# The last 64 tokens of two batches mixed in the two column halves of TensorE's array, with refitted load estimates

## Chip, core and metric

One core of a Trainium2 chip. The metric is the device time of one execution in microseconds. Engine names: PE is TensorE, PEld its weight loads, DVE is VectorE, ACT is ScalarE, POOL is GpSimd, SP is SyncE.

## The reference, cut to what matters

Eight batches of 576 tokens go through block-causal attention (8 heads of 64), and the result x through a mixer:

```python
h = np.maximum(xt @ w_tok1, 0.0) @ w_tok2      # xt: x with tokens and channels swapped
u = x + h.transpose(0, 2, 1)                   # token mixing: 576 tokens <- 256 hidden
h2 = np.maximum(u @ w_ch1, 0.0) @ w_ch2        # channel mixing
return u + h2
```

Token mixing has 576 output tokens, which are 4 chunks of 128 and a rest of 64. The rests of two batches (a pair) share one tile of 128 rows, `um`, so that channel mixing treats them as one more chunk.

## The kernel before

All work is put down as operations with a cost, a priority and dependencies; a list scheduler in the kernel then lays them out, and the order that it finds is the program order of every engine. Loads count in it with an estimated transfer time (`xfer`). The rest of each batch is mixed alone, by two matmuls with the whole array. Of their 128 output rows only 64 are used; the weights are padded with zeros, or shifted by 64 columns for an odd batch, so that the used rows lie where `um` wants them:

```python
for si in range(4 if b == 0 else 0, 5):            # si == 4 is the rest of 64 tokens
    def emit(o, si=si, bank=bank):
        c0 = 128 * si - (64 if si == 4 and odd else 0)
        for t in range(NDT):                       # NDT = 2 halves of the contraction
            nc.tensor.matmul(out=bank_of(bank), lhsT=w2_sb[:, t, c0 : c0 + 128],
                             rhs=at[:, t, :], start=(t == 0), stop=(t == NDT - 1))
    op = P.add("PE", mm_cost(512, 2), emit, ...)
    # then VectorE: u (or 64 rows of um) = bank + x
```

The attention scores use the array in another way: four heads lie in four groups of 32 rows, and their matmuls run side by side. The scheduler knows this as `mode=1` and charges 0.1 us for each change of mode. And at the start PE is given work on zeros (16 matmuls of 512 columns, then smaller ones) to raise its clock before the first scores.

The softmax here doesn't subtract the row's maximum and nothing guards it: scores larger than these inputs give would overflow.

Of the kernel before, what the change touches and what calls it, by code (L numbers as in the profile page):

```python
# [152 lines left out]
def kernel(  # L153
# [53 lines left out]
    zeros = sb.tile([128, 512], BF16, name="zeros")  # L207
    w1_sb = sb.tile([128, 5, DT], BF16, name="w1_sb")
    w1o_sb = sb.tile([128, DT], BF16, name="w1o_sb")
    w2_sb = sb.tile([128, NDT, 640], BF16, name="w2_sb")  # L210
    wc1_sb = sb.tile([128, NDM, DC], BF16, name="wc1_sb")
    wc2_sb = sb.tile([128, NDC, DM], BF16, name="wc2_sb")

# [36 lines left out]
    def init_tiles():  # L250
        def fill(engine, key, prio, *parts):
            for t, value in parts:
                def emit(o, t=t, value=value):
                    (nc.vector if engine == "DVE" else nc.gpsimd).memset(t, value)

                pads.setdefault(key, []).append(P.add(engine, 0.17, emit, (), prio))

        for i, t in enumerate(kT):
            fill("DVE", ("kT", i), -1e4 + i, (t[:, S:640, :], 0.0))
        for i in range(2):  # L260
            fill(
                "DVE", ("v", i), -60 + 20 * i,
                (v1[i][64:128, 4, :, :], 0.0),
                (v1[i][:, 0:4, :, 64:65], 1.0),
                (v1[i][0:64, 4, :, 64:65], 1.0),
            )
            fill("DVE", ("e", i), -70, (e_sb[i][:, :, 1536:1600], 0.0))
            fill("DVE", ("et", i), -70, (et_sb[i], 0.0))
            fill("DVE", ("um", i), -70, (um_sb[i], 0.0))
        fill("DVE", "zeros", -1e5, (zeros, 0.0))  # L270
        fill("DVE", "w1", -70, (w1_sb[64:128, 4, :], 0.0), (w1o_sb[0:64, :], 0.0))
        fill("DVE", "w2", -70, (w2_sb[:, :, S:640], 0.0))

        def emit(o):
            make_identity(nc, ident)

        pads["ident"] = [P.add("POOL", 0.6, emit, (), -1e6)]
# [39 lines left out]
    def load_qk(b, hg, after=[]):  # L317
        i = (2 * b + hg) % 3
        first = b == 0 and hg == 0
        prio = 10 * b + 4 * hg - (100 if b == 0 else 0)  # L320
        parts = ((0, NB // 2), (NB // 2, NB))
        done = []
        for n, (src, raw, dst) in enumerate(((k, kraw[i], kT[i]), (q, qraw[i], qT[i]))):
            hbm = src[b, 4 * hg : 4 * hg + 4].rearrange("h (p k) d -> (h p) (k d)", p=32)
            raw2 = raw.rearrange("p k d -> p (k d)")

            st = stage[0][:, 1152 * n : 1152 * (n + 1)]
            raw_war = reuse(("raw", n, i))
            T_war = reuse(("T", n, i))
            loads = []  # L330
            if not first:
                def emit_load(o, hbm=hbm, raw2=raw2):
                    nc.gpsimd.dma_start(out=raw2, in_=hbm)  # L333

                loads = [P.add("POOL", 0.55, emit_load, raw_war, prio + n, xfer=8 * 0.191)]
            for f, (k0, k1) in enumerate(parts):
                if first:
                    def emit_load(o, k0=k0, k1=k1, hbm=hbm, st=st):
                        queue = nc.sync if o.engine == "SP" else nc.scalar
                        queue.dma_start(out=st[:, D * k0 : D * k1], in_=hbm[:, D * k0 : D * k1])  # L340

                    ld = P.add(("SP", "ACT")[f % 2], 0.45, emit_load, (), -1e4 + n, xfer=(k1 - k0) * 0.1)

                    def emit_cast(o, k0=k0, k1=k1, raw2=raw2, st=st):
                        cast(o, raw2[:, D * k0 : D * k1], st[:, D * k0 : D * k1])

                    w = D * (k1 - k0)
                    ld = P.add(EVAC, {"ACT": act_cost(w), "DVE": dve_cost(w)}, emit_cast, [ld], -1e4 + 2 + n)
                    reads(("g", 0), ld)
                    loads = [ld]  # L350

                def emit(o, raw2=raw2, dst=dst, k0=k0, k1=k1):
                    nc.vector.transpose(  # L353
                        dst[:, 0:S, :]
                        .rearrange("p s e -> p (s e)")
                        .bitcast(I32)
                        .rearrange("p (a k) -> p k a", k=NB)[:, k0:k1],
                        raw2.bitcast(I32).rearrange("p (k a) -> p k a", k=NB)[:, k0:k1],
                    )

                op = P.add("DVE", 0.02 + 32 * (k1 - k0) * 0.00185, emit, loads + T_war + after, prio + 0.1 * n, urgent=(2, 0)[b] if b < 2 else -1)
                reads(("raw", n, i), op)
                done.append(op)
        return done

    def load_v(b):
# [5 lines left out]
        for hg in range(2) if b == 0 else (None,):  # L372
            hs = slice(0, H) if hg is None else slice(4 * hg, 4 * hg + 4)
            nh = hs.stop - hs.start
            for J in range(5):
# [7 lines left out]

                prio = (10 * b + (0, 5.7, 6)[min(b, 2)] if b else (-95.5, 5.15)[hg]) + 0.01 * J
                sw = reuse(("gs", J)) if staged and b else [] if staged else war
                op = P.add("POOL", 0.66 + 0.02 * nh, emit, sw, prio, xfer=p * nh / 16 * (0.0175 if staged else 0.0145))
                if staged:
                    def emit(o, st=st, dst=dst):
                        cast(o, dst, st)
# [8 lines left out]
    def load_token_weights():  # L398
        def load(dst, src, xfer, prio):
            def emit(o):  # L400
                nc.gpsimd.dma_start(out=dst, in_=src)

            return P.add("POOL", 0.66, emit, (), prio, xfer=xfer)

        done1 = [
            load(w1_sb[:, 0:4, :], moe_w_tok1[0:512, :].rearrange("(c p) t -> p c t", p=128), 32 * 0.06, 5.0),
            load(w1_sb[0:64, 4, :], moe_w_tok1[512:576, :], 4 * 0.06, 5.1),
        ]
        done2 = [
            load(w2_sb[:, :, 0:S], moe_w_tok2.rearrange("(p c) s -> p c s", c=2), 8 * 0.3, 5.2)  # L410
        ]
        done1o = [load(w1o_sb[64:128, :], moe_w_tok1[512:576, :], 4 * 0.06, 12.0)]
        return (done1 + pads["w1"], done1 + done1o + pads["w1"]), done2 + pads["w2"]

    def channels(cc):

# [2 lines left out]
    def load_channel_weights():  # L419
        done1, done2 = [[] for _ in range(NDC)], []  # L420
        for f in range(2):
            for m in range(NDM):
                def emit(o, m=m, f=f):
# [1 line left out]
                        out=wc1_sb[:, m, 768 * f : 768 * f + 768],  # L425
                        in_=moe_w_ch1[128 * m : 128 * (m + 1), 768 * f : 768 * f + 768],
                    )
                op = P.add("POOL", 0.53, emit, (), (6.0, 11.5)[f], xfer=0.98)
                for cc in range(0, 8) if f == 0 else range(4, NDC):
                    done1[cc].append(op)  # L430
        for c in range(0, NDC, 4):
# [330 lines left out]
    def token_mix(b, x_done, w1_ready, w2_ready):  # L762
# [4 lines left out]
        a_war = reuse(("a", b % 2))  # L767
        u_war = reuse(("u", b % 3))
        if not odd:
            um_free[pair] = reuse(("um", pair % 2)) + pads["um", pair % 2]  # L770
        uT_war = reuse(("uT", b % 2))
        u_done, done, um_done = [], [], []
        if b == 0:
# [6 lines left out]
        else:  # L780
            a_all = [
                token_up(b, slice(0, DM), (tt,), x_done, a_war, w1_ready, prio) for tt in range(NDT)
            ]
        for si in range(4 if b == 0 else 0, 5):
            bank = {}

            def emit(o, si=si, bank=bank):
                c0 = 128 * si - (64 if si == 4 and odd else 0)
                for t in range(NDT):
                    nc.tensor.matmul(  # L790
                        out=bank_of(bank),
                        lhsT=w2_sb[:, t, c0 : c0 + 128],
                        rhs=at[:, t, :],
                        start=(t == 0),
                        stop=(t == NDT - 1),
                    )

            op = P.add(
                "PE", mm_cost(512, 2), emit,
                a_all + w2_ready + (um_free[pair] if si == 4 else u_war), prio + 1 + 0.1 * si,  # L800
                take=[(BANK, bank)],
            )
            reads(("a", b % 2), op)

            def emit(o, si=si, bank=bank):
                if si < 4:
                    r, dst = slice(0, 128), ut[:, si, :]
                else:
                    r = slice(64, 128) if odd else slice(0, 64)
                    dst = umt[r, :]  # L810
                nc.vector.tensor_tensor(out=dst, in0=bank_of(bank)[r, :], in1=xt[r, si, :], op=ADD)  # L811

            op = P.add("DVE", dve_cost(512), emit, [op], prio, give=[bank])
            reads(("x", b % 3), op)
            u_done.append(op)


        crossbar = b >= 2
# [10 lines left out]
        if crossbar and odd:  # L829
            def emit(o):  # L830
                nc.sync.dma_start_transpose(out=umT[pair % 2], in_=umt)

            op = P.add("SP", 1.0, emit, [u_done[4]] + reuse(("umT", pair % 2)) + um_first[pair], prio, xfer=1.0)
            reads(("um", pair % 2), op)
            um_done.append(op)
        for si in () if crossbar or b == 0 else range(4 + odd):
# [7 lines left out]
                        ps[:, 128 * m : 128 * (m + 1)], src[:, 128 * m : 128 * (m + 1)], ident  # L844
                    )

            deps = [u_done[si]] + pads["ident"]
            deps += uT_war if si < 4 else reuse(("umT", pair % 2)) + um_first[pair]
            op = P.add(
                "PE", mm_cost(128, 4), emit, deps, prio + 2 + 0.1 * si, take=[(BANK, bank)]  # L850
            )
# [11 lines left out]
                EVAC, {"ACT": act_cost(512), "DVE": dve_cost(512, 2)}, emit, [op], prio, give=[bank]  # L863
            )
            (done if si < 4 else um_done).append(op)
        if not odd:
            um_first[pair] = [u_done[-1]]
        return done, um_done, u_done

    um_first = {}  # L870
    um_free = {}


# [161 lines left out]
    for b in range(B + 1):  # L1035
# [7 lines left out]
            )  # L1043
        if b > 0:
            p = b - 1
            uT_done, um_done, u_done = token_mix(p, x_done[p], w1_ready, w2_ready)
            g_done = channel_up(p, uT_done, wc1_ready, 10 * p + 2)
            if p < B - 1:
                channel_down(p, g_done, wc2_ready, u_done, 10 * p + 4)
            if p % 2 == 1:  # L1050
                gm_done = channel_up_mixed(p // 2, um_done, wc1_ready, 10 * p + 3.5)
                prio = 10 * p + (5 if p < B - 1 else 3.9)
                channel_down(p, gm_done, wc2_ready, u_done, prio, mixed=True)
            if p == B - 1:
                channel_down(p, g_done, wc2_ready, u_done, 10 * p + 4)

# [33 lines left out]
```

## Time and profile before

| | before |
|---|---|
| median of the first 3 runs | 308.82 us (308.43 to 308.92) |
| median of those and the 3 beside the changed kernel | 308.63 us |
| span in the profile | 306.6 us |
| PE busy | 97% |
| mixing matmuls of rests | 16, each 0.216 us of PE's stream |
| changes between whole array and score sets | 118 |

The profile's lines are shown and read in the prediction.

### The profile page before, as it was taken

To read this page: it belongs to the slowest core of one execution; us is meant where nothing else is said; L and a number is where in the kernel's file an instruction comes from. 1 tells how busy PE (TensorE), PEld (TensorE's weight loads), DVE (VectorE), ACT (ScalarE), POOL (GpSimd) and SP (SyncE) were. 2 spreads that over 40 slices of the span, in tenths; PEclk is the share of its full clock that TensorE was granted. 3 is DMA by queue.
4 is the path that set the end of the run, shared out by engine and by line. 5 is a ranking of instruction groups with operands and counts; after the bars stand their busy time and mean duration, and the time that the engine had idled before them with its cause. 6 is when DMAs were issued, how large, how long until landed. Compare 5 with 4: busy or idle time off the path is not lost.

```text
span 306.6 us, 7153 instructions
## 1 busy us (share of the span) xinstructions
PE 298.7 (97%) x3007; PEld 162.1 (53%) x3036; DVE 154.6 (50%) x384; ACT 164.2 (54%) x232; POOL 62.1 (20%) x96
## 2 busy tenths in 40 slices
PE   8999999999999999999999999999999999999995
PEld 4575446464564554545545565455445645545643
DVE  6655719898684758856749545281033012011022
ACT  5885864767756645785674884505405602604600
POOL 8866353702600421330050000000000000000000
PEclk9999999999999999999999999999999999999999
DMA  8999999995994798793193030122311312111013
GB/s 201 157 200 208 206 189 181 227 214 88 112 127 74 148 139 135 129 99 71 68 81 87 0 71 2 71 77 45 66 71 71 69 68 83 22 68 72 0 34 138
DMA packets 64512, 31.95 MB, mean 104 GB/s; under 512 B 53088, under 2 KB 55264, under 8 KB 64480
## 3 DMA queue, kind: packets, MB, share of 16 engines
q0 software_dynamic: 44448, 17.34, 48.9%
q1 hardware_dynamic: 19744, 13.57, 16.3%
q10 hardware_dynamic: 288, 0.59, 0.6%
q8 instruction: 23, 0.38, 0.5%
q14 instruction: 9, 0.07, 0.1%
HBM read 35.85 MB, written 9.44 MB: 148 GB/s over the span
## 4 chain that ended last, share of the span: by engine, by line
PE 90%; DVE 6%; DMA 1%; issue 1%; ACT 1%; DVEq 0%
PE mm L966 28%; PE mm L882 27%; PE sc L468 9%; PE mm L515 8%; PE mm L696 6%; PE mm L790 5%; PE mm L909 4%; DVE kT L353 1%; DVE qT L353 1%; DMA gT<-in_k_dram 1%; DVE x_sb L543 1%; PE mm L740 0%; ACT e_sb L487 0%; PE mm L292 0%; PE mm L843 0%
## 5 line engine op out<-in xcount | busy, mean ns | idle before, releaser
L487 ACT ACTIVATE e_sb<-sc 128x1024 bf16<-128x1024 f32 x95 | 92.4, 1026 | 35.8 <-PE sc L468 35.0
L882 PE MATMUL mm<-uT,wc_sb 128*128 128x512 bf16 x384 | 88.5, 380 | 0.1
L966 PE MATMUL mm<-wc_sb,gT 128*128 128x512 bf16 (+1 forms) x378 | 86.3, 373 | 1.5 <-issue 0.8
L682 ACT ACTIVATE gT<-mm 128x512 bf16<-128x512 f32 x75 | 44.8, 597 | 64.6 <-PE mm L882 63.6
L882 PEld LDWEIGHTS <-wc_sb 128*128 128x128 bf16 x384 | 42.2, 114 | 39.7 <-issue 3.5
L966 PEld LDWEIGHTS <-gT 128*128 128x128 bf16 x396 | 36.8, 98 | 42.1 <-issue 4.2
L991 DVE TENSOR_TENSOR o_sb<-mm,u_sb 128x512 f32<-128x512 f32 (+1 forms) x29 | 19.5, 672 | 63.4 <-PE mm L966 63.0
L382 POOL DMA_DIRECT2D v<-in_v_dram x45 | 36.7, 836 | 25.9 <-PE sc L468 22.1
L468 PE MATMUL sc<-qT,kT 32*128 32x320 bf16 (+4 forms) x744 | 35.4, 281 | 1.1 <-DVE qT L353 1.0
L515 PEld LDWEIGHTS <-e_sb 128*128 128x128 bf16 x896 | 30.9, 97 | 7.8 <-issue 4.3
L515 PE MATMUL mm<-v,e_sb 128*128 128x65 bf16 x896 | 33.0, 193 | 0.2 <-DVE x_sb L543 0.2
L543 DVE TENSOR_TENSOR x_sb<-mm,rinv 128x320 bf16<-128x320 f32 x64 | 30.4, 487 | 1.7
L468 PEld LDWEIGHTS <-kT 32*128 32x128 bf16 x752 | 12.4, 93 | 19.8 <-issue 17.2
L493 DVE MEMSET e_sb<- 64x128 uint32 (+1 forms) x72 | 10.5, 153 | 24.3 <-ACT e_sb L487 20.9
L353 DVE STREAM_TRANSPOSE kT<-kraw 128x288 int32<-128x288 int32 x32 | 20.8, 707 | 3.6 <-PE sc L468 2.1
L811 DVE TENSOR_TENSOR u_sb<-mm,x_sb 128x512 bf16<-128x512 f32 x28 | 17.6, 684 | 9.0 <-PE mm L790 7.4
L353 DVE STREAM_TRANSPOSE qT<-qraw 128x288 int32<-128x288 int32 x32 | 21.0, 704 | 0.2
L696 PE MATMUL mm<-x_sb,w_sb 128*128 128x512 bf16 (+1 forms) x99 | 17.9, 314 | 0.3
L684 DVE TENSOR_SCALAR gT<-mm 128x512 bf16<-128x512 f32 x21 | 14.5, 689 | 6.8 <-PE mm L882 6.8
L790 PE MATMUL mm<-aT,w_sb 128*128 128x512 bf16 x70 | 17.7, 379 | 0.1
L333 POOL DMA_DIRECT2D kraw<-in_k_dram x15 | 8.3, 557 | 46.9 <-DVE kT L353 39.8
L537 DVE RECIPROCAL rinv<-mm 128x5 f32<-128x5 f32 x64 | 11.3, 184 | 7.5 <-PE mm L515 7.2
(66 smaller groups left out, 168.3 us busy)
## 6 DMA issues: line engine op xcount, KB each, us to landing
out_dram<-o_sb SPq DMA_DIRECT2D x15, 512.0 KB, 2.8
kraw<-in_k_dram POOLq DMA_DIRECT2D x15, 288.0 KB, 7.2
qraw<-in_q_dram POOLq DMA_DIRECT2D x15, 288.0 KB, 7.1
v<-in_v_dram POOLq DMA_DIRECT2D x28, 128.0 KB, 6.1
wc_sb<-in_moe_w_ch_dram POOLq DMA_DIRECT2D x8, 192.0 KB, 7.5
wc_sb<-in_moe_w_ch_dram POOLq DMA_DIRECT2D x3, 512.0 KB, 10.9
out_dram<-o_sb SPq DMA_DIRECT2D x10, 128.0 KB, 2.3
v<-in_v_dram POOLq DMA_DIRECT2D x15, 64.0 KB, 5.5
```

The source lines that it names most:

```text
L353: nc.vector.transpose(dst[:, 0:S, :] .rearrange("p s e -> p (s e)") .bitcast(I32) .rearrange("p (a k) -> p k a", k=NB)[:, k0:k1], raw2.bit ...
L382: nc.gpsimd.dma_start(out=dst, in_=src)
L468: nc.tensor.matmul(out=home(n)[:, c0 : c0 + w], lhsT=kT[i][r, j0 : j0 + 128, par], rhs=qT[i][r, i0 : i0 + w, par], start=(par == 0), stop= ...
L487: nc.scalar.activation(dst, sc[SC.index(note["pool"])][:, :, 0:n], EXP, scale=scale)
L515: nc.tensor.matmul(out=u[:, I, 0:65], lhsT=w, rhs=vt[:, J, head, 0:65], start=(J == 0), stop=(J == I),)
L543: nc.vector.tensor_tensor(out=xt[:, :, 64 * head : 64 * head + 64], in0=u[:, :, 0:64], in1=ri.to_broadcast([128, 5, 64]), op=MULT,)
L682: nc.scalar.activation(dst, src, RELU)
L696: nc.tensor.matmul(out=bank_of(bank)[:, w * n : w * n + w], lhsT=wt[:, tt : tt + 255 : 2], rhs=xt[:, c, cols], start=(c == 0), stop=(c == 4),)
L790: nc.tensor.matmul(out=bank_of(bank), lhsT=w2_sb[:, t, c0 : c0 + 128], rhs=at[:, t, :], start=(t == 0), stop=(t == NDT - 1),)
L882: nc.tensor.matmul(out=bank_of(bank), lhsT=wc1_sb[:, m, channels(cc)], rhs=uT[b % 2][:, :, m, :], start=(m == 0), stop=(m == NDM - 1),)
L966: nc.tensor.matmul(out=ps, lhsT=gt[:, cc, c0 : c0 + 128], rhs=wc2_sb[:, cc, cols], start=(cc == 0 and not turned), stop=(cc == NDC - 1),)
L991: nc.vector.tensor_tensor(out=dst, in0=ps, in1=(ut if mixed else ut[:, si, :])[:, cols], op=ADD)
```

## The change

The intent: let the two rests of a pair share the array, the even batch's in output columns 0 to 63 and the odd one's in 64 to 127, at the same time and into one bank. Four narrow matmuls should then cost two slots. The even batch's rest now waits for the odd batch. Apart from this, the durations of loads in the scheduler are refitted, which gives another order of instructions. The core of the diff:

```diff
-    w2_sb = sb.tile([128, NDT, 640], BF16, name="w2_sb")
+    w2_sb = sb.tile([128, NDT, S], BF16, name="w2_sb")
 ... (the fills of w2's padding and of um go)
-                loads = [P.add("POOL", 0.55, emit_load, raw_war, prio + n, xfer=8 * 0.191)]
+                loads = [P.add("POOL", 0.55, emit_load, raw_war, prio + n, xfer=8 * 0.184)]
 ... (v: 0.0145 to 0.013 a row and head, w_tok2: 0.3 to 0.25, w_ch1: 0.98 to 0.96)
-        for si in range(4 if b == 0 else 0, 5):
+        for si in range(4 if b == 0 else 0, 4):
 ...
+        if not odd:
+            a_even[pair] = a_all
+        else:
+            def emit(o, bank=bank):
+                for t in range(NDT):
+                    for i in range(2):
+                        nc.tensor.matmul(
+                            out=bank_of(bank)[64 * i : 64 * i + 64, :],
+                            lhsT=w2_sb[:, t, 512:576],
+                            rhs=aT[i][:, t, :],
+                            start=(t == 0),
+                            stop=(t == NDT - 1),
+                        )
+            op = P.add(
+                "PE", mm_cost(512, 2) + 0.02, emit, a_even[pair] + a_all + w2_ready + um_free[pair], prio + 1.4,
+                take=[(BANK, bank)], mode=2,
+            )
 ... (then two VectorE adds of 64 rows, one after the other)
```

More of the change, by code (lines that the diff above doesn't have):

```diff
@@ L268, in init_tiles @@
             fill("DVE", ("et", i), -70, (et_sb[i], 0.0))
-            fill("DVE", ("um", i), -70, (um_sb[i], 0.0))
         fill("DVE", "zeros", -1e5, (zeros, 0.0))
         fill("DVE", "w1", -70, (w1_sb[64:128, 4, :], 0.0), (w1o_sb[0:64, :], 0.0))
-        fill("DVE", "w2", -70, (w2_sb[:, :, S:640], 0.0))
         def emit(o):
@@ L385, in load_v @@
                 sw = reuse(("gs", J)) if staged and b else [] if staged else war
-                op = P.add("POOL", 0.66 + 0.02 * nh, emit, sw, prio, xfer=p * nh / 16 * (0.0175 if staged else 0.0145))
+                op = P.add("POOL", 0.66 + 0.02 * nh, emit, sw, prio, xfer=p * nh / 16 * (0.0175 if staged else 0.013))
                 if staged:
@@ L409, in load_token_weights @@
         done2 = [
-            load(w2_sb[:, :, 0:S], moe_w_tok2.rearrange("(p c) s -> p c s", c=2), 8 * 0.3, 5.2)
+            load(w2_sb, moe_w_tok2.rearrange("(p c) s -> p c s", c=2), 8 * 0.25, 5.2)
         ]
         done1o = [load(w1o_sb[64:128, :], moe_w_tok1[512:576, :], 4 * 0.06, 12.0)]
-        return (done1 + pads["w1"], done1 + done1o + pads["w1"]), done2 + pads["w2"]
+        return (done1 + pads["w1"], done1 + done1o + pads["w1"]), done2
     def channels(cc):
@@ L427, in emit @@
                     )
-                op = P.add("POOL", 0.53, emit, (), (6.0, 11.5)[f], xfer=0.98)
+                op = P.add("POOL", 0.53, emit, (), (6.0, 11.5)[f], xfer=0.96)
                 for cc in range(0, 8) if f == 0 else range(4, NDC):
@@ L769, in token_mix @@
         if not odd:
-            um_free[pair] = reuse(("um", pair % 2)) + pads["um", pair % 2]
+            um_free[pair] = reuse(("um", pair % 2))
         uT_war = reuse(("uT", b % 2))
@@ L783, in token_mix @@
             ]
-        for si in range(4 if b == 0 else 0, 5):
+        for si in range(4 if b == 0 else 0, 4):
             bank = {}
             def emit(o, si=si, bank=bank):
-                c0 = 128 * si - (64 if si == 4 and odd else 0)
                 for t in range(NDT):
@@ L791, in emit @@
                         out=bank_of(bank),
-                        lhsT=w2_sb[:, t, c0 : c0 + 128],
+                        lhsT=w2_sb[:, t, 128 * si : 128 * si + 128],
                         rhs=at[:, t, :],
@@ L799, in token_mix @@
                 "PE", mm_cost(512, 2), emit,
-                a_all + w2_ready + (um_free[pair] if si == 4 else u_war), prio + 1 + 0.1 * si,
-                take=[(BANK, bank)],
+                a_all + w2_ready + u_war, prio + 1 + 0.1 * si, take=[(BANK, bank)],
             )
@@ L805, in emit @@
             def emit(o, si=si, bank=bank):
-                if si < 4:
-                    r, dst = slice(0, 128), ut[:, si, :]
-                else:
-                    r = slice(64, 128) if odd else slice(0, 64)
-                    dst = umt[r, :]
-                nc.vector.tensor_tensor(out=dst, in0=bank_of(bank)[r, :], in1=xt[r, si, :], op=ADD)
+                nc.vector.tensor_tensor(out=ut[:, si, :], in0=bank_of(bank), in1=xt[:, si, :], op=ADD)
             op = P.add("DVE", dve_cost(512), emit, [op], prio, give=[bank])
@@ L815, in token_mix, with emit @@
             u_done.append(op)
+        um_rows = []
+        if not odd:
+            a_even[pair] = a_all
+        else:
+            bank = {}
+            def emit(o, bank=bank):
[12 more added lines that the diff above has]
+            )
+            for i in range(2):
+                reads(("a", i), op)
+                r = slice(64 * i, 64 * i + 64)
+                def emit(o, i=i, r=r, bank=bank):
+                    nc.vector.tensor_tensor(
+                        out=umt[r, :], in0=bank_of(bank)[r, :], in1=x_sb[(b - 1 + i) % 3][r, 4, :], op=ADD
+                    )
+                um_rows.append(P.add("DVE", dve_cost(512), emit, [op] + um_rows, prio, give=[bank] if i else ()))
+                reads(("x", (b - 1 + i) % 3), um_rows[-1])
         crossbar = b >= 2
@@ L831, in emit @@
                 nc.sync.dma_start_transpose(out=umT[pair % 2], in_=umt)
-            op = P.add("SP", 1.0, emit, [u_done[4]] + reuse(("umT", pair % 2)) + um_first[pair], prio, xfer=1.0)
+            op = P.add("SP", 1.0, emit, um_rows + reuse(("umT", pair % 2)), prio, xfer=1.0)
             reads(("um", pair % 2), op)
@@ L845, in emit @@
                     )
-            deps = [u_done[si]] + pads["ident"]
-            deps += uT_war if si < 4 else reuse(("umT", pair % 2)) + um_first[pair]
+            deps = ([u_done[si]] if si < 4 else um_rows) + pads["ident"]
+            deps += uT_war if si < 4 else reuse(("umT", pair % 2))
             op = P.add(
@@ L865, in token_mix @@
             (done if si < 4 else um_done).append(op)
-        if not odd:
-            um_first[pair] = [u_done[-1]]
-        return done, um_done, u_done
-    um_first = {}
+        return done, um_done, u_done, um_rows
+    a_even = {}
     um_free = {}
@@ L1045 @@
             p = b - 1
-            uT_done, um_done, u_done = token_mix(p, x_done[p], w1_ready, w2_ready)
+            uT_done, um_done, u_done, um_rows = token_mix(p, x_done[p], w1_ready, w2_ready)
             g_done = channel_up(p, uT_done, wc1_ready, 10 * p + 2)
@@ L1052 @@
                 prio = 10 * p + (5 if p < B - 1 else 3.9)
-                channel_down(p, gm_done, wc2_ready, u_done, prio, mixed=True)
+                channel_down(p, gm_done, wc2_ready, um_rows, prio, mixed=True)
             if p == B - 1:
```

## The prediction

> **What bounds the kernel now.** I read the page's busy shares first, then the slices, then what TensorE (PE) waits for, then the chain that ended last. In the first two:
>
> ```profile
> PE 298.7 (97%) x3007; PEld 162.1 (53%) x3036; DVE 154.6 (50%) x384; ACT 164.2 (54%) x232; POOL 62.1 (20%) x96
> ...
> PE   8999999999999999999999999999999999999995
> ...
> PEclk9999999999999999999999999999999999999999
> ...
> PE 90%; DVE 6%; DMA 1%; issue 1%; ACT 1%; DVEq 0%
> PE mm L966 28%; PE mm L882 27%; PE sc L468 9%; PE mm L515 8%; PE mm L696 6%; PE mm L790 5%; PE mm L909 4%; DVE kT L353 1%; DVE qT L353 1%; DMA gT<-in_k_dram 1%; DVE x_sb L543 1%; PE mm L740 0%; ACT e_sb L487 0%; PE mm L292 0%; PE mm L843 0%
> ```
>
> PE is over 90% busy in every slice but the first and last, at full clock; every other engine is near half. The chain is 90% PE. PE's own waits in the whole run, in the view of who waited for whom, are four lines:
>
> ```profile
> PE mm L285 <- DVE zeros L254: 1.2, 1, 1.2
> PE sc L468 <- DVE qT L353: 1.0, 2, 0.6
> PE mm L966 <- issue: 0.8, 5, 0.2
> PE mm L515 <- DVE x_sb L543: 0.2, 1, 0.2
> ```
>
> So from about 8 us on, the time is the sum of what PE is given. A busy record of PE is wider than its place in the stream (379 ns for one 512-column matmul), so I take the place from the chain, which counts start to start:
>
> ```profile
> 209.87 8.63 PE mm L882 x40
> ...
> 290.39 12.94 PE mm L966 x71
> ```
>
> 8.63 us / 40 = **0.216 us** for a 512-column matmul on the whole array, whatever its rows or columns fill. The mixing matmuls that the change touches are these, in the groups with shapes kept apart:
>
> ```profile
> L790 PE MATMUL mm<-aT,w_sb 128*128 128x512 bf16 x70 | 17.7, 379 | 0.1
> ```
>
> (72 in the program; two records are missing.) They wait for nothing and stand on the path: 5% of the chain.
>
> **What the skill says.** (1) "TensorE: Matmul & The Clock Gate", Back-to-back issue gap: N/2.4 + 2.5 ns when warm, 216 ns for 512 columns. The trace agrees (0.216). (2) "TensorEngine Tiling (Array Packing)", Key Properties: changing the tiling mode drains the array. The trace agrees: in the 59 pairs of changes between whole-array matmuls and the row-tiled scores, the first matmul of the new mode starts a median 0.096 us late when entering the tiled mode and 0.096 us when leaving it, beyond the slot of the matmul before (from start times of single matmuls). (3) The same page, Restrictions: column tiling turns the fast weight load off. All 3036 weight loads before are 128 columns wide, so this trace cannot show it. (4) The first page again, Part 3: three column tiles with 32 columns and N=512 gave 2.38 times the throughput. No column tile is in the kernel before; row tiles are, and they run side by side (four starts within 10 ns).
>
> **The change part by part.**
> Removed: before, the last 64 tokens of each batch are mixed by two whole-array matmuls whose output is half unused: 8 batches x 2 = 16 matmuls x 0.216 = 3.45 us of PE. Added: per pair of batches four matmuls with 64 output columns, two contraction halves times two column halves, in one bank: 16 again (the order of the built programs confirms 72 whole-array mixes becoming 56 plus 16 of 64x512). If the two halves run side by side, a block costs two slots.
>
> The best yardstick in the trace is a score set with eight matmuls of 512 columns in two rounds. Start to start:
> - entry 0.095 us;
> - first to second round 0.240 us, that is 0.024 over a slot;
> - from the first matmul of the set to the first after it 0.564 us (median of 14 sets).
>
> So such a block takes 0.095 + 0.564 = 0.659 us where four whole-array matmuls take 0.863 us: **0.204 us saved a block, 0.82 us for four.** The chain bears this out with neighbouring pieces:
>
> ```profile
> 29.71 2.71 PE mm L882 x12
> 32.42 0.57 PE sc L468 x15
> 32.99 2.72 PE mm L882 x12
> 35.71 0.57 PE sc L468 x16
> ```
>
> From 29.71 to 32.99 is 3.28 us; 12 x 0.216 = 2.59 leaves 0.69 for a set whose two rounds stream 1024 columns, 0.43 us: 0.26 us over for the mode changes and joints (this set has four rounds of parts, so slightly more than the 0.23 above).
>
> One of the four blocks stands directly before a score set in the built order, so it shares a change: there are 125 mode changes after, 118 before, seven more rather than eight. That gives back 0.095: **0.91 us** in sum. The loss of fast weight load pulls the other way. The first loads of a block cannot be hidden behind the block before it, and a slower one might expose some 0.03 us (my guess from a 0.098 us whole load, of which part is latency): 4 x 0.03 = 0.1. Net of the blocks: **-0.8 us**.
>
> Adds: eight VectorE adds of 64 rows before and after, 0.68 us each; they only come later, two in a row. VectorE is half idle. The removed fills of the padding (two of 0.272 us at 1.8 to 2.6 us, and one for the weights) lie before the first k load has landed: nothing. The token weights now load whole rows; PE waits for no DMA: nothing.
>
> Order: the new load estimates move instructions. The one place that I can weigh is the stall at 28.5 us (0.51 us beyond a slot and a mode change), where the chain runs through VectorE:
>
> ```profile
> 26.58 0.37 DVE uT L757
> ...
> 27.19 0.67 DVE um_sb L811
> 27.86 1.18 DVE qT L353 x2
> ```
>
> In the new order batch 0's last 64 tokens are not mixed here, and VectorE does neither this add nor the last cast of uT before the q transposes. They can start when the q load has landed, about 25.1 us (GpSimd's next issue, released by that load, is at 25.2). The scores come straight after the first mix, so their wait mostly goes; but ScalarE now does the fourth cast of uT (about 26.7 to 27.3 us, after its third), and the channel matmuls will wait some 0.3 us for it. Worth -0.2. Against it: in the first pair the PE transposes of the shared tile now wait for four plain adds and two serial ones, 6 x 0.68 = 4.1 us of VectorE, with only about 2.2 us of PE work between the block and those transposes: perhaps +0.2. I let them cancel, and give the rest of the shuffle -0.2 with no good reason beyond fewer banks taken (four fewer of the 512-column kind).
>
> Sum: 308.8 - 0.8 - 0.2 = **307.8 us**.
>
> **Rivals.**
> (a) The column halves do not run side by side. Both halves read all 128 rows of two different tensors, unlike the score sets, which read 32 rows each; the trace shows no such case. A block then costs 4 x 0.216 + 0.095 + 0.024 + 0.1 = 1.08 us against 0.863: +0.22 each, +0.8 after the shared change: 309.6. For it: the missing fast load and the doubled reading. Against: (4) above. I give it 15%.
> (b) A new wait. The shared tile's mix and both adds now come with the odd batch, and the mixed channel matmuls hang on them. In three pairs the transposing DMA lands 2.5 us after issue and over 5 us of other PE work lies before its user in the new order, so nothing shows. In the first pair PE transposes: a few tenths at most. If earlier scores outrun their transposes or loads, each such place costs 0.3 to 0.6 us, as at 28.5 us now; two of them would eat the gain: 308.8.
> (c) The load estimates are the main thing, and the kernel gains more than the blocks give. Speaks against it: all of PE's waits after 8 us sum to about 2 us, half of it issue, and no wait names a DMA. At most 1 us more: 306.8.
>
> **Range and chances.** The main story gives 307.8 with 0.4 of scheduling either way; (a) reaches 309.6, (c) 306.8. The three runs before spread 0.5 us. Range 306.8 to 309.1. Two per cent is 6.2 us, more than all removed matmuls and all waits together (3.45 + 2), so faster by over 2%: 1%; slower by over 2% would need a stall of a kind that the trace doesn't hold: 1%; same 98%.
>
> **What would show it.** Right: the 64x512 matmuls start in two rounds of two, the two of a round within some 50 ns, rounds about 0.24 us apart, block to next about 0.66 us with entry; 56 whole-array mixes; PE's waits still near 3 us in all; no wait at the 28 us scores. Wrong: four starts 0.216 us apart (a); or a new wait of PE on the um adds, umT or q and k transposes of over 0.5 us (b); or a span shorter by over 2 us, which would mean that I mis-sized the drains or missed a stall.

## More of the kernel before

One view of its beginning is needed later: PE in order of time, with start and duration in us.

```profile
1.19 5.20 PE L285 MATMUL mm<-zeros 128*128 128x512 bf16 x16 [1.19 <-DVE zeros L254]
6.23 1.58 PE L292 MATMUL mm<-zeros 128*128 128x256 bf16 x13
8.39 0.32 PE L468 MATMUL sc<-qT,kT 32*128 32x320 bf16 x2 [0.58 <-DVE qT L353]
```

PE has done its start-up work early and waits 0.58 us for q's transposes. Everything after 8.39 us is the long PE stream.

## The result, and the profile after

The changed kernel took a median of **307.09 us** (306.82 to 308.40, 6 runs) beside 308.63 us (308.12 to 309.75, 6 runs). The ratio is 0.9954, with a 95% interval of 0.993 to 0.9978. Ratios here are the mean time of one kernel's runs over that of the other's in the same rounds, so not quite the ratio of the medians quoted. At 2% it is the same; it is a real half per cent. A second set of rounds in a later session (after_again below) gave 307.42 us and a ratio of 0.9955.

The page of the changed kernel, in the same parts as shown for the kernel before:

```profile
PE 298.9 (98%) x3005; PEld 160.7 (53%) x3035; DVE 153.2 (50%) x379; ACT 165.1 (54%) x234; POOL 61.9 (20%) x96
...
PE 96%; DVE 2%; issue 1%; ACT 0%
PE mm L989 30%; PE mm L905 28%; PE mm L513 10%; PE sc L466 10%; PE mm L694 6%; PE mm L787 4%; PE mm L932 4%; PE mm L283 2%; PE mm L290 1%; PE mm L818 1%; PE mm L738 0%; ACT e_sb L485 0%; DVE u_sb L802 0%; DVE um_sb L835 0%; DVE x_sb L541 0%
```

PE remains the bound, and now carries 96% of the chain in place of 90%: VectorE has nearly left it. L787 and L818 are the mixing. PE's waits, by whom it waited for (us in total, times, longest):

```profile
PE mm L283 <- DVE zeros L254: 1.2, 1, 1.2
PE mm L989 <- issue: 0.8, 5, 0.2
PE mm L513 <- DVE e_sb L491: 0.2, 1, 0.2
```

The wait of the scores for q's transposes has gone. The groups with shapes kept apart show the two kinds of mixing matmul, the second with 64 columns:

```profile
L787 PE MATMUL mm<-aT,w_sb 128*128 128x512 bf16 x53 | 13.5, 379 | 0.2
L818 PE MATMUL mm<-aT,w_sb 128*64 128x512 bf16 x16 | 2.5, 391 | 0.0
```

A group's busy time counts overlapping matmuls once. So 16 records of 391 ns make 2.5 us, and that alone says that they overlap: before, 70 records of 379 ns made 17.7 us, in which 16 of them have 16/70 x 17.7 = 4.0 us. (The program has 56 whole-array mixes; three records are missing.) One block in order of time:

```profile
156.33 1.04 PE L989 MATMUL mm<-wc_sb,gT 128*128 128x512 bf16 x4
157.30 0.62 PE L818 MATMUL mm<-aT,w_sb 128*64 128x512 bf16 x4
157.86 0.82 PE L989 MATMUL mm<-wc_sb,gT 128*128 128x512 bf16 x3
```

From 157.30 to 157.86 is 0.56 us for four matmuls. The starts of the single matmuls in the trace are 0, 3, 240 and 243 ns: two rounds of two. All four blocks agree: 0.093 us of delay on entry, 0.555 us from the first matmul to the next one after the block, together 0.648 us. The four whole-array matmuls of before took 4 x 0.216 = 0.863 us.

The chain around the scores of batch 1, where the kernel before had its stall (start, us, what):

```profile
26.42 0.86 PE mm L738 x4
27.29 0.56 PE sc L466 x8
27.85 2.71 PE mm L905 x12
```

There is no VectorE piece left. But the two profiled executions hide part of the gain, because they began differently. The changed kernel's beginning:

```profile
1.19 6.51 PE L283 MATMUL mm<-zeros 128*128 128x512 bf16 x16 [1.19 <-DVE zeros L254]
7.54 1.58 PE L290 MATMUL mm<-zeros 128*128 128x256 bf16 x13
9.05 0.32 PE L466 MATMUL sc<-qT,kT 32*128 32x320 bf16 x2
```

The same 16 matmuls on zeros took 6.51 us in place of 5.20: at first the starts of these matmuls are 427 ns apart, later 216, so PE begins at half rate; in this execution the last matmul at half rate ended at 7.1 us, in the one before at 4.5 us. The first scores, behind them in program order, started 0.66 us later although q had been ready. The two profiled executions are not average ones. Each run lists the span, the time from the first to the last instruction. The profiled execution of the changed kernel, with 305.9 us, is the longest of six (305.0 to 305.9, mean 305.38); that of the kernel before, with 306.6, lies under the mean of the others of that kernel (306.80 and 306.72 in the two sessions below). So the mean spans differ by 1.3 to 1.4 us, and these two by 0.7. To leave the start out, I compare the stretch from the first score matmul to the last matmul, by start times in the trace: **294.65 us before, 293.27 after, 1.38 us less**, and account for it. A slot is the time from the start of one matmul to that of the next in a steady stream (0.216 us for 512 columns); a filler is a matmul on zeros of 256 columns.

| term | us | how |
|---|---|---|
| whole-array matmuls removed | -3.45 | 16 x 0.216 |
| blocks added | +1.83 | 4 x (2 x 0.216 + 0.024 between rounds) |
| mode changes, 118 to 125 | +0.67 | 7 x 0.096 |
| one start-up filler fewer after the first scores | -0.11 | 256 columns |
| waits of PE, 1.12 to 0.77 | -0.34 | see below |
| sum | -1.40 | measured: -1.38 |

The first three are the blocks: **-0.95**. The waits are summed from start times: every matmul that starts over 35 ns later than its predecessor's slot (and a mode change, where there is one) allows, left out where a record is missing. They come out larger than in the view of waits, whose busy records are wider than a slot. The line "issue: 0.8, 5" in that view is no waiting: these are five places where a matmul's record is missing, and the profile of after_again, which has 3035 records in place of 3005, has no such line. Gone are 0.51 us at 28.3 us, 0.17 at 56.2 and 0.27 at 115.7, all three behind VectorE. New are 0.30 us at 16.4 (attention's outputs, on a mask by VectorE), 0.09 at 46.5, and the transposes of the first pair's shared tile, which wait 0.35 us in place of 0.16.

### The profile page after: what moved, and what is told of

It reads as the page before. It is cut to its first block, busy times and chain, and to the rows that moved or that the text cites. A ratio compares the mean times of both kernels' runs of the same rounds, so it can differ in the third digit from the quotient of the medians.

```text
span 305.9 us, 7148 instructions
## 1 busy us (share of the span) xinstructions
PE 298.9 (98%) x3005; PEld 160.7 (53%) x3035; DVE 153.2 (50%) x379; ACT 165.1 (54%) x234; POOL 61.9 (20%) x96
## 4 chain that ended last, share of the span: by engine, by line
PE 96%; DVE 2%; issue 1%; ACT 0%
PE mm L989 30%; PE mm L905 28%; PE mm L513 10%; PE sc L466 10%; PE mm L694 6%; PE mm L787 4%; PE mm L932 4%; PE mm L283 2%; PE mm L290 1%; PE mm L818 1%; PE mm L738 0%; ACT e_sb L485 0%; DVE u_sb L802 0%; DVE um_sb L835 0%; DVE x_sb L541 0%
## 5 line engine op out<-in xcount | busy, mean ns | idle before, releaser
L466 PEld LDWEIGHTS <-kT 32*128 32x128 bf16 x752 | 12.1, 93 | 19.2 <-issue 16.4
L682 DVE TENSOR_SCALAR gT<-mm 128x512 bf16<-128x512 f32 x22 | 15.2, 689 | 10.7 <-PE mm L905 10.6
L680 ACT ACTIVATE aT<-mm 128x512 bf16<-128x512 f32 (+1 forms) x15 | 8.1, 541 | 15.3 <-PE mm L694 15.1
```

Source lines behind the costliest of these rows:

```text
L466: nc.tensor.matmul(out=home(n)[:, c0 : c0 + w], lhsT=kT[i][r, j0 : j0 + 128, par], rhs=qT[i][r, i0 : i0 + w, par], start=(par == 0), stop= ...
L680: nc.scalar.activation(dst, src, RELU)
```

## Experiments

Eight runs, each with 5 timed rounds beside the kernel before; the results were correct in all. Medians of before in the two sessions: 308.57 and 308.60 us (11 runs each). First scores, stretch and waits are of the one profiled execution, as above; the mean span is over all six executions of a run (11 for before). A time is 1.7 to 3.0 us longer than its span, so medians also carry what happens before the program's first and after its last instruction.

| run | median us | mean span us | ratio to before (95%) | first scores at us | stretch us | waits in it us |
|---|---|---|---|---|---|---|
| before | 308.57, 308.60 | 306.80, 306.72 | 1 | 8.39 | 294.65 | 1.12 |
| blocks_only | 308.09 | 306.27 | 0.9981 (0.9969 to 0.9994) | 8.81 | 293.98 | 1.33 |
| loads_only | 307.84 | 306.07 | 0.9973 (0.9957 to 0.999) | 8.16 | 294.46 | 1.07 |
| halves_in_turn | 307.66 | 305.55 | 0.9965 (0.9951 to 0.998) | 8.92 | 293.31 | 0.79 |
| warm12 | 307.06 | 305.25 | 0.9946 (0.9933 to 0.9958) | 8.12 | 293.66 | 1.12 |
| after_again | 307.42 | 305.40 | 0.9955 (0.9934 to 0.9977) | 8.68 | 293.33 | 0.83 |
| tails_alone | 309.61 | 308.05 | 1.0038 (1.0015 to 1.006) | 8.28 | 295.99 | 0.70 |
| block_by_scores | 307.21 | 305.35 | 0.9951 (0.9932 to 0.9969) | 8.25 | 293.67 | 1.42 |
| both_tuned | 306.52 | 304.78 | 0.993 (0.9911 to 0.9948) | 8.23 | 292.94 | 0.69 |

### The blocks without the new load estimates (blocks_only)

```diff
 (the changed kernel)
-xfer=8 * 0.184 ... 0.013 ... 8 * 0.25 ... 0.96
+xfer=8 * 0.191 ... 0.0145 ... 8 * 0.3 ... 0.98
```

> The changed kernel with the old load estimates: the column-half blocks alone. Theory (blocks give 0.96 us by starts in the trace; the rest of the gain of 1.5 us is the stall of 0.5 us at the scores of 28 us, which goes because batch 0's add is no longer ahead of the q transposes): 1.2 to 1.5 us faster than the kernel before, no wait of PE on qT near 28 us, blocks of 0.65 us each. Rival (the refitted load estimates give most of it): under 0.8 us faster, with the stall at 28 us still there.

Neither came out whole. The blocks are 0.65 us each and the wait on qT is gone, as my theory said, but the gain is only 0.5 us in the median and the mean span, and 0.67 us in the stretch. The chain shows where the rest went:

```profile
65.99 0.72 DVE kT L351
66.71 0.03 DVE rinv L535
66.77 0.50 DVE x_sb L541
67.27 0.04 issue
67.31 0.38 PE mm L868 x4
```

L868 at 67.31 us are PE's transposes of the first pair's shared tile. This order puts them behind attention work that VectorE delays, and PE starts them 0.60 us late. With 0.37 us before the channel matmuls at 27.7 us, on VectorE's cast of uT, and the old stall of 0.17 us at 56 us, the waits sum to 1.33 us in place of 1.12: -0.95 + 0.21 = -0.74, measured -0.67. So in this execution the blocks gave all they have to give, and the order took some of it back.

### The load estimates without the blocks (loads_only)

```diff
 (the kernel before)
-xfer=8 * 0.191 ... 0.0145 ... 8 * 0.3 ... 0.98
+xfer=8 * 0.184 ... 0.013 ... 8 * 0.25 ... 0.96
```

> The kernel before with the new load estimates alone. Theory: the order puts the q transposes ahead of batch 0's add, so the stall at 28 us goes too: 0.4 to 0.6 us faster than the kernel before, all 72 mixes still whole-array and 118 mode changes. Rival (the estimates are the main thing): over 1 us faster. A second rival (estimates do nothing): same within 0.2 us, stall still 0.5 us.

The median and the mean span fell by 0.7 us, but the stretch of the one profiled execution by only 0.19. That execution also began 0.23 us earlier than the profiled one of before (8.16 against 8.39 us), and its span is 0.4 us shorter; where the other executions gain more is not shown, since they left no trace. In the profiled one the wait at the scores of batch 1 did not go, as it should have by my theory. It is 0.41 us beyond a slot and a mode change:

```profile
26.39 0.45 PE mm L790 x2
26.83 0.03 DVEq L811
26.87 0.26 DVE qT L353
27.13 0.04 issue
27.17 0.64 PE sc L468 x8
```

Here q's transposes are ahead of the um add, as in the changed kernel, yet PE comes to the scores so early that they are not done: in this execution k's transposes began at 24.73 us, on k's load. So the stall depends on when PE gets there and when the load lands. What the estimates do in this stretch is 0.11 us for a filler less and 0.05 us of waits, together 0.16, measured 0.19.

The two single effects on the stretch, 0.67 and 0.19 us, do not add to 1.38, and the column of waits says why: 1.33 and 1.07 us with one part each, 0.77 and 0.83 with both. But these are single executions. The mean spans fall by 0.53 and 0.73 us with one part each and by 1.3 to 1.4 with both, which does add up within the noise (the 95% interval of each single difference is about 0.36 us either way). So over all executions the new estimates alone are worth about as much as the blocks alone; that the two parts help each other is not shown.

### The pairing taken apart in program order (halves_in_turn)

```diff
 (the changed kernel)
-                for t in range(NDT):
-                    for i in range(2):
+                for i in range(2):
+                    for t in range(NDT):
```

> The changed kernel with the four matmuls of a block in another order: both contraction halves of the even batch, then both of the odd one. Same instructions, same mode changes, only the pairing is lost in part. Theory (the gain of a block is that matmuls of different column halves that follow each other start together): three rounds in place of two, so block to next 0.22 us longer, 4 x 0.22 = 0.86 us slower than the changed kernel, about 0.7 us faster than the kernel before. Rival (the hardware finds the pairs by itself, whatever the order): same as the changed kernel. Another rival (the gain is from the mode or from the smaller blocks): same as the changed kernel.

The first rival holds and my theory falls. The stretch is 293.31 us against 293.27 and 293.33 in the two profiles of the changed kernel, and a block looks the same:

```profile
156.21 1.04 PE L989 MATMUL mm<-wc_sb,gT 128*128 128x512 bf16 x4
157.18 0.63 PE L818 MATMUL mm<-aT,w_sb 128*64 128x512 bf16 x4
157.74 1.04 PE L989 MATMUL mm<-wc_sb,gT 128*128 128x512 bf16 x4
```

The single starts are 0, 7, 240 and 247 ns. Two matmuls of one column half start 240 ns apart where they are alone (tails_alone, below), so a start 7 ns after the first must belong to the other half: the hardware started the third matmul of the program before the second. The waits confirm it: in this block the built program puts a wait for ScalarE on the third and the fourth matmul; in the trace it is on the second and the fourth to start. (In the changed kernel's program that wait is on the second and the fourth, and there too on the second and the fourth to start.) The median, 307.66, lies inside the range of the changed kernel's runs on the other chip (306.79 to 307.97), and the mean span, 305.55 us, is within 0.2 us of the changed kernel's. The other rival, that the gain is from the mode or from narrower matmuls, expected the same result here; tails_alone decides about it.

### Narrow matmuls, each batch alone (tails_alone)

```diff
 (the kernel before)
-                        out=bank_of(bank),
-                        lhsT=w2_sb[:, t, c0 : c0 + 128],
+                        out=bank_of(bank)[half, :],          # 64 rows, by odd or even
+                        lhsT=w2_sb[:, t, c0 : c0 + width],   # 64 columns
```

> The kernel before, with each batch's last 64 tokens mixed by matmuls of 64 output columns in a column half, but each batch alone, as before. Same 16 matmuls, no pairing. Theory (only the pairing saves; narrow matmuls take a whole slot, and each separate block pays two mode changes of 0.096 us and a joint of about 0.02): 133 mode changes in place of 118, so 15 x 0.096 + 8 x 0.02 = 1.6 us slower than the kernel before. Rival (a narrow matmul is itself cheaper, or a change between whole array and column halves costs little): same or faster.

The stretch grew by 1.34 us. Its waits happen to be 0.42 us shorter than before; with them put back the growth is 1.76 us, against 1.6 expected. The median is 1.0 us higher, the mean span 1.33. A block of one batch has starts at 0 and 240 ns and takes 0.093 + 0.552 = 0.645 us, the same as 0.648 for two batches in one. The groups say it too:

```profile
L792 PE MATMUL mm<-aT,w_sb 128*128 128x512 bf16 x56 | 13.7, 380 | 0.0
L792 PE MATMUL mm<-aT,w_sb 128*64 128x512 bf16 x16 | 5.0, 391 | 0.0
```

The 16 narrow matmuls fill 5.0 us here and 2.5 us in pairs. So a narrow matmul is not cheaper and the mode alone gains nothing; the second half of the array is free, and the mode changes have to be paid out of that.

### The changed kernel once more (after_again)

> The changed kernel once more, on the chip of the three next to it. From the first scores to the last matmul it took 293.27 us in its profile (294.65 before): the same to 0.1 us is expected, since nothing there is left to chance. The start should vary: the first scores at 8.1 to 9.1 us by when PE's clock rises. Median 1.2 to 1.6 us under the kernel before.

No edit. The stretch repeats to 0.06 us (293.33), the first scores came at 8.68 us in place of 9.05, and the gain over before was 1.2 us. The two medians of the changed kernel, 307.09 and 307.42 us, differ by 0.3 us, but the mean spans are 305.38 and 305.40, so most of that difference lies outside the span and not in the start. The stretch repeated here because no wait on a load fell into it; loads_only, warm12 and block_by_scores show that one can.

### Fewer matmuls on zeros (warm12)

```diff
 (the changed kernel)
-            for _ in range(WARM):
+            for _ in range(12):
```

> The changed kernel with 12 in place of 16 of the matmuls on zeros at the start, the order otherwise the same. In the profile of the changed kernel PE was still at half rate until 6.8 us (3.9 us in the profile before), so the 16 and the 13 smaller ones after them ended only at 9.05 us, though the q transposes had ended at 8.1 us. Theory: the first scores start at 8.1 to 8.4 us whenever the clock rises, so the median falls by 0 to 0.9 us, about 0.4, and the spread of runs shrinks. Rival (fewer matmuls leave the clock low for longer): scores at half rate after 8 us, 0.5 us or more slower.

(The times of the clock in the expectation are rough; 7.1 and 4.5 us, as above, are the ends of the last matmul at half rate.) The start did what was expected: 8.12 us, and six runs from 306.82 to 307.26, a spread of 0.4 us where the changed kernel had 1.6 and 1.2. (Only a part of this is the start: the spans reach from 305.0 to 305.5 us here and from 305.0 to 305.9 in both sets of the changed kernel.) But 0.39 us of it was lost at the scores of batch 1, which came too early for q's load. The median, 307.06, is not clear of the changed kernel's.

### Blocks after score sets (block_by_scores) and both (both_tuned)

```diff
 (the changed kernel, in the scheduler's choice)
+                    if o.mode == 2 and mode != 1 and t < o.ready + 4.0:
+                        continue
+                    rank = (-o.urgent, not (o.mode == 2 and mode == 1), o.prio, o.n)
```

> The changed kernel, with the blocks held back (up to 4 us) until a score set has just ended: three of four then follow a score set, and the mode changes fall from 125 to 123. Theory: 2 x 0.096 = 0.19 us less from the first scores to the last matmul, if the shuffle adds no wait; in the median that is hardly to be told from noise. Rival (a change between two tiled modes costs more than one between a tiled mode and the whole array): no gain.

> As block_by_scores, with 12 in place of 16 start-up matmuls as well. Theory: the first scores at 8.1 us; the early start is partly given back at the first scores of batch 1 (about 27 us), which wait for q's transposes, as in warm12 (0.4 us); so 0.1 to 0.5 us faster than the changed kernel, and a smaller spread. Rival: the same as the changed kernel, since what is gained at the start is all lost at 27 us.

Alone, the shuffle shows nothing in the median (307.21), and its stretch is longer because of one wait of 0.73 us at the scores of batch 1, whose k load landed late in that execution (k's transposes began at 24.75 us, released by the load; in both_tuned at 23.78). Without that wait it would be 292.94 us. With the shorter start-up added, the wait was absent, and 292.94 us is what the stretch measures: 0.39 us under the changed kernel's 293.33, of which 2 x 0.096 = 0.19 is mode changes and 0.14 the waits. The median is **306.52 us** (306.38 to 307.03), 0.9 us under the changed kernel beside it (0.6 in the mean span) and the best of all kernels here. That is more than the 0.1 to 0.5 us expected, because the wait that was to give part of it back did not come. Against before it is 0.993, against 0.9955 for the changed kernel in the same rounds; the intervals just overlap. Its beginning in time:

```profile
1.19 5.28 PE L286 MATMUL mm<-zeros 128*128 128x512 bf16 x12 [1.19 <-DVE zeros L257]
6.29 1.60 PE L293 MATMUL mm<-zeros 128*128 128x256 bf16 x13
8.22 0.32 PE L469 MATMUL sc<-qT,kT 32*128 32x320 bf16 x2 [0.33 <-DVE qT L354]
```

PE again waits for q's transposes and not the other way round. Why the loads of batch 1 land up to a microsecond apart in different executions stays open: warm12 and both_tuned have the same order up to there, and one profile has 0.39 us of wait and the other none.

## Why the prediction was right

The time, 307.8 us with a range of 306.8 to 309.1, was met, though both medians, 307.09 and 307.42, lie under its centre: the steps sum to -1.0 us, and the stretch shows -1.4. The step that was off most is the stall at 28.5 us. By its steps:

- **PE's stream sets the time.** Right. Slots, joints, mode changes and waits explain the stretch of every kernel here to within 0.2 us of what they measured against before.
- **The blocks, -0.8 us.** Right in mechanism, a little short: -0.95. The entry (0.093 in place of 0.095), the time from round to round (0.240, of which 0.024 is the joint beyond a slot) and the block to its successor (0.555 in place of 0.564) are those of the score sets taken as yardstick. The term that was mis-sized is the slower weight load: narrow loads do take longer (106 to 109 ns for 64 columns, 98 for 128), but nothing of the 4 x 0.03 us came to the surface. The shared mode change was found as counted.
- **The stall at 28.5 us, -0.2 us.** Mis-sized. In the two profiles of the changed kernel all of the 0.51 us went, or all but 0.06, so -0.5. The 0.3 us of waiting for the last cast of uT showed in no trace of this order, not even in both_tuned, which began at 8.23 us; why it stayed away is not shown. loads_only, warm12 and block_by_scores show that 0.4 to 0.7 us of waiting can come back at these scores, on a load that lands late and not on the add. All three began early (8.12 to 8.25 us), but so did both_tuned, without such a wait.
- **The first pair's transposes, +0.2 us.** Right: 0.35 us of wait in place of 0.16. With the old load estimates (blocks_only) PE came to them 0.60 us late, behind attention work on VectorE and not behind the adds.
- **The rest of the shuffle, -0.2 us "with no good reason".** There were reasons that I did not read out of the profile: two more waits behind VectorE, 0.17 us at 56.2 and 0.27 us at 115.7, at the end of stretches in which the chain before runs through VectorE. I read the sums of PE's waits but not the chain there. Against them stand the new 0.30 us at 16.4 us and 0.09 us, so the waits of this term came to nothing; one filler fewer gave 0.11. The prediction's "half of it issue" was no waiting either, but missing records; without them the view of waits has 1.4 us after the change, where the prediction's sign of being right had "near 3 us in all".
- **Rival (a), the halves not side by side.** Refuted by the starts of 0 and 3 ns; tails_alone shows that without pairing the same narrow matmuls cost time. **Rival (b), a new wait,** is what happens to blocks_only. **Rival (c), the estimates are the main thing and the kernel gains more than the blocks give:** the second half is right, by 0.4 us (-1.4 against -0.95). The first half is open: alone the estimates give 0.19 us of one stretch but 0.73 us of the mean span, against 0.53 for the blocks alone; on top of the blocks they give 0.7 us of the stretch (293.98 to 293.27) and 0.9 of the mean span. The prediction dismissed them because few waits stood in one profile.
- Not foreseen: the start. "At full clock" is not so for the first 3.3 us of matmuls before, which ran at half rate (427 ns from start to start in place of 216); the page's clock line does not show it. The first scores of the two profiles of the changed kernel are 0.38 us apart for this reason, and spans of one kernel reach over up to 1.0 us, as much as the blocks are worth; how much of that is the start and how much the loads of batch 1 is not shown.

## What to carry to other kernels

Half-empty matmuls are worth pairing in the column halves even in a kernel that is bound by PE alone: a pair costs what one half costs, but a separate block pays about 0.2 us for two mode changes and a joint, about one whole-array slot (0.216 us), so it has to save more than one; here it saves two. Put such a block next to work that has left the plain mode anyway. And where a few tenths of a per cent matter, cut the stretch from the first real matmul to the last out of the trace and count it, but hold it against the spans of all executions: a single time here carries 1.7 to 3.0 us from outside the span, and a single stretch carried 0.4 to 0.7 us from when a load landed.

## What the Trainium skill lacked or had wrong

- "TensorE: Matmul & The Clock Gate", Part 3, The mechanism, says that matmuls start in strict program order. With column halves they do not: in halves_in_turn two matmuls of each half stand behind each other in the program, and the starts are 0, 7, 240 and 247 ns, with the third of the program second. The block takes 0.65 us in either order.
- "TensorEngine Tiling (Array Packing)", Key Properties, says that a change of mode drains the array but not what it costs: about 0.09 us here (0.093 from the whole array into column halves, a median 0.096 into and out of row tiles, 0.087 to 0.091 from row tiles to column halves), and 0.024 us more between the two rounds of a tiled set.
- The same page, Restrictions, says that column tiling turns the fast weight load off, but not what that costs. The loads then took 106 to 109 ns for 64 columns against 98 ns for 128, and none of it showed in the time of a block.
- "TensorE: Matmul & The Clock Gate", Part 1, What you observe, puts the rise of the clock at around 4 us of sustained activity, 0.5 us either way from run to run. In the eight profiles here with 16 start-up matmuls PE's rate doubled 3.3 to 5.9 us after the first matmul.
